# A fused attention and feed-forward block on one core: 32 loads moved to ScalarE's queue, 13 warm-up products instead of 17, and a new written-out order

## The chip, the cores and the metric

The kernel runs on one core of a Trainium2 chip. The metric is the device time of one execution in microseconds (us), lower is better. The kernel before was run three times for its time, and once more with the hardware profiler on. The core has a matrix engine (TensorE, PE in the profile, with its weight loads shown as PEld), a vector engine (VectorE, DVE), a scalar engine (ScalarE, ACT), GpSimd (POOL), and a sync engine (SyncE, SP) that in the kernel before issues all the transfers between memory and the on-chip buffers. Each engine works through its own list of instructions in order; between engines, semaphores hold an instruction back until what it needs is done.

## The reference

One transformer block over 2048 rows of width 576, in bf16: layer norm, a linear-memory attention with 32 heads of width 18 in four segments of 512 rows, an output projection with residual, a second layer norm, and a feed-forward layer of width 4608 with GELU, with residual.

```python
def _A_ref(x, wq, wk, wv, wo, beta):
    # q, k, v = x @ wq, x @ wk, x @ wv, cut into 32 heads and N = 4 segments of L = 512 rows
    g = _sigmoid(beta).reshape(1, H, 1, 1)
    for s in range(N):
        logits = jnp.einsum('bhqd,bhkd->bhqk', qs, ks) * scale + mask
        a_dot = jnp.einsum('bhqk,bhkd->bhqd', _softmax(logits, axis=-1), vs)
        pq = phi(qs)                       # phi(t) = t + 1 where t > 0, else exp(t)
        a_mem = (pq . M) / (pq . z + 1e-06)
        outs.append(g * a_mem + (1.0 - g) * a_dot)
        M = M + einsum(phi(ks), vs); z = z + sum(phi(ks))
    return o @ wo

def _B_ref(x, w1, b1, w2, b2):
    h = _gelu(jnp.einsum('bsd,df->bsf', x, w1) + b1)
    return jnp.einsum('bsf,fd->bsd', h, w2) + b2

h = x + _A_ref(_layernorm(x), ...)
h2 = h + _B_ref(_layernorm(h), ...)
```

## The kernel before

The 2048 rows are cut into 16 tiles of 128 rows (`t`) and 8 chunks of 256 rows (`c`, two tiles each). For a tile, `project` loads its rows (`load_x`, L263), normalises them (`layernorm`), turns them (by TensorE for the first three tiles, L409, by a transposing transfer L154 for the others), and multiplies by wq, wk and wv in column chunks `ch` (L350 is the main part over 4 x 128 rows of the weights, L354 the fifth part of 64 rows, padded with zeros). Chunks 0 and 1 hold 432 columns of q and k, chunk 4 the other 144 columns of both (288 together). `copies` (L502 to L515) takes the products out of the accumulators into `qk_pad` and `v_aug`. Heads are turned once more into `QT` and `KT` (L531, L534). `attend` multiplies scores (L623, 32 rows of the array each, four side by side), takes exp on ScalarE (L627), masks on GpSimd (L631), and weighs values (L639). `output` multiplies by wo, adds the residual, and normalises again. The feed-forward layer follows: `first_layer` (L350 again, with `w1g`, `hT` or `wqkv` as weight buffers, evictions L769 to L771, GELU L792) and `second_layer` (L852, with the residual rows `hc` read back at L843).

The weights of the first feed-forward layer don't stay on the chip: for each group of 512 columns, `load_w1` issues one load of 512 KB (L726) and two of 32 KB (L729, the 64-row rest in two halves, called tails here), into buffers whose last reader must be done. `dma` gives every transfer to SyncE's list.

At the start of the program TensorE has nothing to multiply until the first rows are loaded and normalised. `zeros` (L333) gives it products of a buffer of zeros: 4 of 512 columns and then 13 of 256 columns (`ZEROS = 17` in all), whose result nobody reads. ScalarE meanwhile zeroes padding with copies from the same buffer (`zero`, L308).

Two 64-row products can run side by side in the two halves of the array. `rest_of` pairs such fifth parts (L443 for the projections, L750 for the feed-forward layer). Numbers in the set `WHOLE` name the pairs that are not made; there the fifth part is a full-height product (L354).

Nothing is scheduled when the kernel is built: every operation gets a number as the code defines it, and the table `ORDER` at the end says in which sequence all operations are issued, which fixes each engine's list. `PLACE` gives each accumulator its bank, `FLIP` names the operations that run on their second engine (`alt`) instead of their first. Up to eight transfers are in flight: each takes the next of eight landing semaphores in turn, and waits until the transfer eight places earlier has landed.

## Time and profile before

| | |
|---|---|
| three timed runs | 451.98, 452.14, 453.31 us; median 452.14 |
| the profiled execution | 452.16 us, of which the span from the first to the last instruction is 450.3 us |
| TensorE busy | 445.4 us of the span (99%) |
| ScalarE, VectorE, GpSimd busy | 331.1, 271.4 and 230.2 us |
| transfers | 78.40 MB, mean 174 GB/s |

The profile page lists busy time per engine, the span in 40 slices, the chain of work that ended last, and the costliest groups of instructions. A row of the timeline gives the start, the busy time, the engine and line, what it writes and reads, the size of the array's part that is used (rows x columns, as 128\*128), the shape of one output, how many equal instructions were merged, and in square brackets the idle time before, with what ended it. "SPq" rows are SyncE's issues of transfers, of which only the issue is in the row. Products overlap in the array, so the spacing of starts says more than the length of one.

### The profile page before, as it was taken

Reading aid. Unit: us, or ns where it says so; the run is one execution under the profiler, and the core shown is the slowest. Engines: PE = TensorE matmul, PEld = TensorE weight load, DVE = VectorE, ACT = ScalarE, POOL = GpSimd, SP = SyncE. Lnnn points to the kernel's source line nnn. Section 1 sums busy time; section 2 is a strip of 40 time slices with the busy share of each in tenths; the row PEclk is TensorE's granted clock in tenths of the full one; section 3 lists DMA queues with packets and bytes.
Section 4 is the critical chain, followed back from the end, with each engine's and each line's share of the span. In section 5 each row is a group of like instructions: output and inputs, shape, how many; then the busy total and the mean of one; then the engine's idle time right before and its main releaser. Section 6 shows DMA issues by size and latency. Waiting matters only on the chain.

```text
span 450.3 us, 14470 instructions
## 1 busy us (share of the span) xinstructions
PE 445.4 (99%) x6090; PEld 331.0 (74%) x6090; DVE 271.4 (60%) x624; ACT 331.1 (74%) x318; POOL 230.2 (51%) x409
## 2 busy tenths in 40 slices
PE   8999999999999999999999999999999999999997
PEld 4556877676776777676777677777877878877886
DVE  7989989887887568666666766665523531311231
ACT  8999999988879977889788878587877162352550
POOL 6888865887884667753664784554341002000000
PEclk9999999999999999999999999999999999999999
DMA  7699989678498567796567957585667466365411
GB/s 204 206 209 243 203 215 274 180 194 162 131 168 228 154 148 196 188 155 188 158 153 173 206 123 170 160 227 157 200 181 194 138 192 196 92 191 172 139 41 52
DMA packets 114353, 78.40 MB, mean 174 GB/s; under 512 B 48832, under 2 KB 112240, under 8 KB 114288
## 3 DMA queue, kind: packets, MB, share of 16 engines
q1 hardware_dynamic: 114288, 77.48, 68.7%
q8 instruction: 47, 0.77, 0.7%
q14 instruction: 18, 0.15, 0.1%
HBM read 60.09 MB, written 7.08 MB: 149 GB/s over the span
## 4 chain that ended last, share of the span: by engine, by line
PE 96%; DMA 2%; SPq 1%; issue 0%; DVE 0%
PE bank L350 30%; PE bank L852 25%; PE st L350 10%; PE st L852 6%; PE st L623 6%; PE bank L639 5%; PE bank L683 3%; PE bank L750 3%; PE bank L354 2%; PE st L683 1%; PE st L750 1%; DMA w1g<-in_B_w_dram 1%; PE bank L593 1%; PE bank L531 1%; DMA wqkv<-in_A_wk_dram 1%; PE bank L561 1%
## 5 line engine op out<-in xcount | busy, mean ns | idle before, releaser
L627 ACT ACTIVATE pt<-st 128x2048 bf16<-128x2048 f32 x80 | 150.2, 1877 | 42.4 <-PE st L623 34.8
L852 PEld LDWEIGHTS <-hT 128*128 128x128 bf16 x1188 | 111.5, 98 | 28.1 <-issue 1.5
L852 PE MATMUL bank<-w_sb,hT 128*128 128x288 bf16 (+1 forms) x936 | 130.2, 284 | 0.0
L631 POOL TENSOR_SCALAR_AFFINE_SELECT pt<-pt 128x512 bf16<-128x512 bf16 x128 | 80.5, 644 | 41.2 <-ACT pt L627 40.8
L350 PEld LDWEIGHTS <-w1g 128*128 128x128 bf16 x944 | 86.7, 98 | 18.7 <-issue 7.2
L350 PE MATMUL bank<-xn2T,w1g 128*128 128x256 bf16 (+1 forms) x728 | 89.6, 268 | 0.0
L771 DVE TENSOR_TENSOR hT<-bank,b1T 128x512 bf16<-128x512 f32 x74 | 50.1, 681 | 37.9 <-PE bank L350 36.6
L792 ACT ACTIVATE hT<-hT 128x1536 bf16<-128x1536 bf16 (+4 forms) x25 | 65.9, 2665 | 0.3 <-DVE hT L771 0.2
L769 ACT ACTIVATE hT<-bank,b1T 128x256 bf16<-128x256 f32 x70 | 28.9, 474 | 31.9 <-PE bank L350 31.8
L350 PE MATMUL bank<-wqkv,xT 128*128 128x432 bf16 (+2 forms) x192 | 40.3, 341 | 0.8 <-DMA wqkv<-in_A_wk_dram 0.6
L350 PEld LDWEIGHTS <-xT 128*128 128x128 bf16 x264 | 23.6, 98 | 19.3 <-issue 2.2
L858 DVE TENSOR_TENSOR ot<-bank,hc 128x288 bf16<-128x288 f32 (+1 forms) x26 | 11.7, 448 | 41.9 <-PE bank L852 38.2
L852 PE MATMUL st<-w_sb,hT 128*128 128x288 bf16 (+1 forms) x252 | 33.0, 277 | 0.0
L623 PE MATMUL st<-QT,KT 32*128 32x128 bf16 x1280 | 32.2, 217 | 0.0
L654 DVE STREAM_TRANSPOSE bank<-bank 128x512 f32<-128x512 f32 x32 | 23.0, 720 | 15.0 <-PE bank L639 14.6
L623 PEld LDWEIGHTS <-KT 32*128 32x128 bf16 x1280 | 18.5, 92 | 16.9 <-issue 12.8
L771 DVE TENSOR_TENSOR hT<-st,b1T 128x512 bf16<-128x512 f32 x25 | 16.7, 681 | 23.1 <-PE st L350 23.1
L588 POOL TENSOR_TENSOR pq<-ek,pq 128x512 bf16<-128x512 bf16 x24 | 28.0, 1168 | 4.3 <-DVE ek L587 3.7
L350 PE MATMUL st<-xn2T,w1g 128*128 128x256 bf16 x216 | 29.4, 273 | 0.0
L657 POOL TENSOR_TENSOR r<-r,omg 128x16 f32<-128x16 f32 x32 | 7.0, 219 | 36.9 <-DVE r L655 34.6
L769 ACT ACTIVATE hT<-st,b1T 128x256 bf16<-128x256 f32 x20 | 8.1, 472 | 21.3 <-PE st L350 21.3
L639 PE MATMUL bank<-pt,v_aug 128*19 128x128 bf16 x1280 | 23.8, 220 | 0.0
(157 smaller groups left out, 664.2 us busy)
## 6 DMA issues: line engine op xcount, KB each, us to landing
w1g<-in_B_w_dram SPq DMA_DIRECT2D x57, 512.0 KB, 4.0
w_sb<-in_B_w_dram SPq DMA_DIRECT2D x12, 432.0 KB, 6.3
wqkv<-in_B_w_dram SPq DMA_DIRECT2D x10, 512.0 KB, 4.6
hd<-h_t SPq DMA_DIRECT2D x16, 288.0 KB, 3.4
hc<-hd SPq DMA_DIRECT2D x32, 144.0 KB, 2.3
w1g<-in_B_w_dram SPq DMA_DIRECT2D x114, 32.0 KB, 3.4
x_b<-in_A_x_dram SPq DMA_DIRECT2D x18, 144.0 KB, 2.8
hT<-in_B_w_dram SPq DMA_DIRECT2D x5, 512.0 KB, 5.2
```

The costliest lines, as they stand in the source:

```text
L350: nc.tensor.matmul(out=acc, lhsT=lhsT_of(slice(0, P), k), rhs=rhs_of(slice(0, P), k), start=start and k == 0, stop=False, skip_group_check ...
L588: op(("m_add", n), "POOL", lambda: nc.gpsimd.tensor_tensor(out=pq[:], in0=e_g, in1=pq[:], op=ALU.add), ["ek"], ["pq"])
L623: nc.tensor.matmul(out=st4[:, i, n * P:(n + 1) * P], lhsT=KTs[(2 * s0 + kt) % NK][rows, g, :], rhs=QTs[(2 * c + qt) % NQ][rows, g, :], sta ...
L627: op(("exp", v), "ACT", lambda pt=pt: nc.scalar.activation(out=pt[:], in_=open_four("scores")[:], func=ACT.Exp, scale=scale), [st], [("pt" ...
L631: op(("mask", v), "POOL", lambda n=n, pt=pt: nc.gpsimd.affine_select(out=pt[:, :, n * P:(n + 1) * P], in_=pt[:, :, n * P:(n + 1) * P], pat ...
L639: nc.tensor.matmul(out=bank(ox)[32 * i:32 * i + E, (g % 4) * P:(g % 4) * P + P], lhsT=v_augs[(2 * s0 + kt) % NV][:, G * i + g, :], rhs=pt[ ...
L654: op(("f_T", n), "DVE", lambda: nc.vector.transpose(out=bank(ox), in_=bank(ox)), [], [ox])
L683: nc.tensor.matmul(out=bank(b)[:, 0:HALF], lhsT=xTt[:, k, :], rhs=wo_t[:, k, hs], start=(k == 0), stop=(k == KT - 1))
L769: nc.scalar.activation(out=dst[:, j, :], in_=acc()[:, j, :], func=ACT.Identity, bias=b1T[:, j0 + j:j0 + j + 1], scale=1.0)
L771: op(name, "DVE", lambda: nc.vector.tensor_tensor(out=dst, in0=acc(), in1=bias, op=ALU.add), [tok, "b1T"], keys, alt=("ACT", by_act), afte ...
L792: op(("gelu", c, f0, f), "ACT", lambda: nc.scalar.activation(out=hT[:, f0:f, :], in_=hT[:, f0:f, :], func=ACT.Gelu_apprx_tanh), [], [("hT" ...
L852: nc.tensor.matmul(out=bank(b)[:, 0:w], lhsT=hT[:, q, tl * P:(tl + 1) * P], rhs=w2_sb[:, q, hs], start=(q == 0), stop=(q == NF - 1))
```

## The change

`dma` gets a second engine: with the operation's number in `FLIP`, the same transfer is issued from ScalarE's list (`by_act`) instead of SyncE's. Transposing transfers are left out of that. `FLIP` names 32 transfers: the rows of tile 0 (`x_p`), `beta`, the 576 columns of `wv`, and 29 later ones: 24 loads of feed-forward weights, four of the residual rows `hc` and one store of `out`. The same eight landing semaphores serve both queues. `ZEROS` goes from 17 to 13, which moves all later numbers by four. `ORDER`, `PLACE` and the other entries of `FLIP` are new, and `WHOLE` has 14 entries instead of 13.

```diff
-    ZEROS = 17
+    ZEROS = 13
...
-    def dma(name, kb, desc, issue, rd=(), wr=(), after=()):
-        o = op(name, "SP", issue, rd, wr, after=after)
+    queue = [nc.sync]
+
+    def dma(name, kb, desc, issue, rd=(), wr=(), after=(), turns=False):
+
+        def by_act():
+            queue[0] = nc.scalar
+            issue()
+            queue[0] = nc.sync
+
+        o = op(name, "SP", issue, rd, wr, None if turns else ("ACT", by_act), after=after)
         o.kb, o.desc = kb, desc
         return o
...
-        dma((name, t), 144, 8, lambda: nc.sync.dma_start(out=dst[:], in_=x[t * P:(t + 1) * P, :]), (), [key])
+        dma((name, t), 144, 8, lambda: queue[0].dma_start(out=dst[:], in_=x[t * P:(t + 1) * P, :]), (), [key])
...
     FLIP = {
-        15, 28, 29, 31, 32, 33, 34, 35, 36, 43, 45, 49, 50, 51, 53, 57, 62, 63, 64, 65, 66, 132, 134, 136, 138, 142,
+        0, 9, 14, 15, 25, 29, 31, 32, 33, 34, 35, 36, 38, 46, 49, 50, 51, 57, 58, 59, 66, 125, 128, 130, 132, 134,
...
     WHOLE = {
-        246, 399, 406, 469, 470, 543, 647, 774, 852, 853, 1501, 2141, 2142,
+        242, 243, 395, 402, 465, 466, 539, 643, 770, 848, 849, 1497, 2137, 2138,
     }
...
     ORDER = [
-        23, 57, 24, 42, 54, 25, 0, 29, 58, 30, 26, 28, 59, 27, 38, 125, 67, 68, 126, 69, 70, 71, 6, 22, 127, 1, 72,
+        0, 25, 23, 47, 4, 1, 67, 35, 22, 57, 26, 68, 33, 69, 58, 59, 7, 24, 52, 121, 32, 60, 14, 70, 122, 3, 29, 71,
```

What the new order does is read from the engines' lists. Line numbers of the changed kernel are 10 higher in the functions concerned. The first place is the start of SyncE's list, here of the kernel before (`x_p0`, `x_p1` are the rows of tiles 0 and 1; `128x4x432` is the main part of 432 columns, `64x...` a fifth part):

```order
L263 DMA x_p0_76<-in_A_x_dram 128x576
L273 DMA wqkv_62<-in_A_wk_dram 128x4x144
L263 DMA x_p1_77<-in_A_x_dram 128x576
L263 DMA x_b0_78<-in_A_x_dram 128x576
L281 DMA beta_bc_61<-in_A_beta_dram 128x32
L277 DMA wqkv_62<-in_A_wq_dram 64x576
L273 DMA wqkv_62<-in_A_wq_dram 128x4x144
L277 DMA wqkv_62<-in_A_wk_dram 64x144
L273 DMA wqkv_62<-in_A_wk_dram 128x4x432
```

The same place on SyncE in the changed kernel:

```order
L287 DMA wqkv_62<-in_A_wq_dram 64x576
L273 DMA x_p1_77<-in_A_x_dram 128x576
L287 DMA wqkv_62<-in_A_wk_dram 64x144
L283 DMA wqkv_62<-in_A_wq_dram 128x4x144
L287 DMA wqkv_62<-in_A_wk_dram 64x432
L283 DMA wqkv_62<-in_A_wk_dram 128x4x144
L283 DMA wqkv_62<-in_A_wk_dram 128x4x432
L273 DMA x_b0_78<-in_A_x_dram 128x576
L283 DMA wqkv_62<-in_A_wq_dram 128x4x432
```

The 432 columns of wk are issued ninth before and seventh now; `x_p0` and `beta` have left this list, and `x_b0` (rows of tile 2) comes after them.

The second place is the start of ScalarE's list up to the copy of tile 0's turned rows, `xT0`, for which TensorE's first real products wait. Before (all `L308` rows zero padding; `g_bc` is the gate computed from beta):

```order
L308 ACT_TABLE_LOAD
L308 COPY phik_pad1_93<-pq_116 128x32x14
L308 COPY hT1_126<-pq_116 64x256
L308 COPY hT0_125<-pq_116 128x32x14
L308 COPY MZ_blk_75<-pq_116 128x512
L308 COPY w1g1_67<-pq_116 64x256
L308 COPY phik_pad0_92<-pq_116 128x32x14
```

```order
L336 ACTIVATE g_bc_71<-beta_bc_61 128x32
L308 COPY hT1_126<-pq_116 64x256
L308 COPY MZ_blk_75<-pq_116 128x512
L413 COPY xT0_84<-bank2_152 128x640
L308 COPY hT0_125<-pq_116 128x32x14
L504 ACTIVATE qk_pad0_148<-bank3_153,rs_early0_127 128x16x18
```

Between these two pieces stand two more `w1g` copies. The same stretch of ScalarE's list now:

```order
L273 DMA x_p0_76<-in_A_x_dram 128x576
L318 ACT_TABLE_LOAD
L318 COPY w1g1_67<-pq_116 64x256
L318 COPY hT1_126<-pq_116 64x256
L291 DMA beta_bc_61<-in_A_beta_dram 128x32
L318 COPY MZ_blk_75<-pq_116 128x512
L318 COPY phik_pad0_92<-pq_116 128x32x14
```

```order
L346 ACTIVATE g_bc_71<-beta_bc_61 128x32
L318 COPY hT1_126<-pq_116 64x256
L318 COPY o_nat1_114<-pq_116 128x4x16
L318 COPY MZ_blk_75<-pq_116 128x512
L423 COPY xT0_84<-st0_213 128x640
L283 DMA wqkv_62<-in_A_wv_dram 128x4x576
```

Between these stand a copy each of `hT1`, `phik_pad1` and `o_nat0`. Three issues have come in, two ahead of the `xT0` copy and one right behind it. The computing instructions ahead of that copy are eleven before and now: the 448-element copy into `hT0` and two of 256 into `w1g` have moved behind it, and one of 256 into `hT1` and two of 64 into `o_nat` have come ahead.

The third place is late in the program (segment four, scores of tile 14), on ScalarE. Before, with `pt` the exp of scores, `ek` an exp for the memory part:

```order
L627 ACTIVATE pt1_110<-st_5783 128x2048
L627 ACTIVATE pt2_111<-st_5783 128x2048
L627 ACTIVATE pt3_112<-st_5783 128x2048
L585 ACTIVATE ek_115<-QT2_102 128x512
L627 ACTIVATE pt0_109<-st_5783 128x2048
```

And now:

```order
L637 ACTIVATE pt1_110<-st_5780 128x2048
L853 DMA hc_123<-hd_147 128x288
L736 DMA w1g0_66<-in_B_w1_dram 128x4x512
L637 ACTIVATE pt2_111<-st_5780 128x2048
L595 ACTIVATE ek_115<-QT2_102 128x512
L637 ACTIVATE pt3_112<-st_5780 128x2048
L739 DMA w1g1_67<-in_B_w1_dram 64x256 x2
L873 DMA out_0_dram<-ot_124 128x576
```

Five transfers now stand between the exps, two of them in one place and three in another. TensorE's list keeps its blocks, in another sequence in the first 70 us and from about 285 us on; its runs of equal array shape number 276 before and 272 now, counted over the whole list, and one pair of fifth parts (of tile 3's chunks 2 and 3) is no longer made, so that two full-height fifth parts of 432 columns take its place.

## The prediction

> **What bounds the kernel now.** I read the page's busy shares first, then the table by stage, then TensorE's timeline where that table shows idle time.

> ```profile
> PE 445.4 (99%) x6090; PEld 331.0 (74%) x6090; DVE 271.4 (60%) x624; ACT 331.1 (74%) x318; POOL 230.2 (51%) x409
> PE 96%; DMA 2%; SPq 1%; issue 0%; DVE 0%
> ...
> 0.00:12.00 12.00, 9.97 (x59) 5.45 (x60) 8.63 (x36) 9.80 (x21) 7.27 (x25) 1.00 0.77 213
> 12.00:115.00 103.00, 103.00 (x1804) 72.71 (x1802) 89.63 (x205) 94.45 (x79) 83.36 (x157) 1.00 0.86 204
> 115.00:285.00 170.00, 170.00 (x2436) 123.45 (x2429) 117.50 (x271) 142.49 (x129) 108.58 (x178) 1.00 0.75 173
> 285.00:430.00 145.00, 144.93 (x1627) 114.68 (x1624) 52.23 (x109) 80.54 (x88) 30.94 (x52) 1.00 0.58 169
> 430.00:450.00 20.00, 17.46 (x179) 14.74 (x176) 3.37 (x7) 3.82 (x5) 0.00 (x0) 1.00 0.16 45
> ```

> TensorE carries 96% of the chain, and in the stage table (first busy column: PE) it has no idle time from 12 to 285 us and 0.07 us from there to 430. After its last product only an addition and the last stores are left, and the change leaves those. So loads, exps and evictions hide behind TensorE today. The change can gain only at the start, in that 0.07 us, or in TensorE's own work; it can lose wherever a cover breaks.

> The start, in TensorE's timeline:

> ```profile
> 1.24 3.38 PE L333 MATMUL bank<-pq 128*128 128x512 bf16 x11 [1.24 <-DVE pq L292]
> ...
> 5.12 1.06 PE L333 MATMUL bank<-pq 128*128 128x256 bf16 x4
> 6.20 0.53 PE L409 MATMUL st<-ident,xn 128*128 128x128 bf16 x5
> 6.57 0.38 PE L333 MATMUL bank<-pq 128*128 128x256 bf16 x2
> 7.16 0.67 PE L350 MATMUL bank<-wqkv,xT 128*128 128x288 bf16 x4 [0.21 <-ACT xT L413]
> 7.66 0.29 PE L354 MATMUL bank<-wqkv,xT 128*128 128x288 bf16 x1
> 7.81 0.66 PE L350 MATMUL st<-wqkv,xT 128*128 128x288 bf16 x4
> ...
> 9.15 0.90 PE L350 MATMUL bank<-wqkv,xT 128*128 128x432 bf16 x4 [0.55 <-DMA wqkv<-in_A_wk_dram]
> ```

> Two waits count: 0.21 us for ScalarE's copy `xT0`, and 0.55 us for the 432 columns of wk. The zero products are in idle time. Of the second wait the chain of waits shows the origin: it runs back through SyncE's issues from the first one on.

> ```profile
> 0.79 0.39 SPq L263
> 1.24 0.42 SPq L273
> 1.72 0.50 SPq L263
> ...
> 3.20 0.56 SPq L277
> 3.81 0.58 SPq L273
> 4.42 0.52 SPq L277
> 4.99 4.12 DMA wqkv<-in_A_wk_dram
> ```

> **The change, part by part.**

> *Loads at the start.* The wk load is issued ninth at 4.99 us and lands 4.12 us later, 9.11. In the new list six issues precede it: three fifth parts at about 0.61, 0.57 and 0.57 us from start to start (3.20 to 3.81, and 4.42 to 4.99), `x_p1` at about 0.5 (the row at 1.72), and two of 144 columns at 0.61 and 0.48 (3.81 to 4.42, 1.24 to 1.72). 0.79 + 3.34 = 4.13; I take 4.2. With the same 4.12 us it lands at 8.3. The rows of tile 0 are again the first on their own queue, so I leave their issue at 0.79 and VectorE's start unchanged. No row shows two queues issuing at once. Below, a gain is excluded, since 0.79 is each engine's first moment; above, the two first issues could go one after the other, which shifts everything on SyncE by that row's 0.39 us and lands wk at 8.7. I take 8.3: 0.39 us spread over two queues is the exception, at two of nine issues.

> [...]

> *ScalarE up to `xT0`.* ScalarE now begins with an issue:

> ```profile
> 0.79 1.28 ACT L308 ACT_TABLE_LOAD   x1 [0.79 <-PEq L1056]
> 2.08 0.56 ACT L308 COPY phik_pad<-pq 128x448 bf16<-128x448 bf16 x1
> 2.55 0.87 ACT L308 COPY hT<-pq 64x256 bf16<-64x256 bf16 x2
> ...
> 3.85 0.40 ACT L308 COPY w1g<-pq 64x256 bf16<-64x256 bf16 x1
> 4.15 0.56 ACT L308 COPY phik_pad<-pq 128x448 bf16<-128x448 bf16 x1
> ...
> 6.42 0.68 ACT L413 COPY xT<-bank 128x640 bf16<-128x640 bf16 x1
> ```

> From 2.08 to 6.42 its eleven instructions take 4.34 us. Gone from ahead of the copy are a 448-wide copy (0.47, from 2.08 to 2.55) and two of 256 (0.30 each, 3.85 to the next start at 4.15); new are one of 256 (0.30) and two of 64 elements, which I put at 0.2 each: 4.34 - 1.07 + 0.70 = 3.97 us. Added are two issues of about 0.4 us each, bounded by 0 (hidden while the engine still copies) and 0.8. The first stands ahead of everything and can't hide; of the second I count half: 0.6. Start of the copy: 2.08 + 3.97 + 0.6 = 6.65, end about 7.3, TensorE's first real product 7.4 instead of 7.16 (+0.2). The two 288-column projections then take 1.3 us (7.16 to 7.81, twice), so the 432-column one starts at 8.7, after wk has landed in either case, instead of 9.15: **-0.45 us**. If ScalarE's issues hide, the copy is at 6.05 and wk's landing at 8.3 decides: -0.85.

> *Behind it on ScalarE.* The wv issue (0.58 at most) and three zero copies (about 0.45, 0.45 and 0.3) stand between `xT0` and the eviction for which the turning of q waits. Before, TensorE turned q at once after its projections (13.08 + 0.18 = 13.26, no idle time), so ScalarE is needed there on time. By the same spacings the eviction ends about 0.1 us late: **+0.1**. wv itself is issued near 7.4, ahead of the first projection's end, so I let its users not wait.

> *Zero products.* Four fewer of 0.21 us in time that is idle anyway: nothing, as long as the idle time itself does no harm (rival 1). What covers the cost is the loading and the layer norm of tiles 0 and 1, which end at the same time.

> *TensorE's order.* The products are the same but for fillers and one pair. A block in another array shape costs at its borders:

> ```profile
> 13.08 0.35 PE L354 MATMUL st<-wqkv,xT 128*128 128x432 bf16 x1
> 13.26 1.06 PE L531 MATMUL bank<-ident,qk_pad 128*128 128x128 bf16 x16
> ...
> 17.42 0.40 PE L623 MATMUL st<-QT,KT 32*128 32x128 bf16 x16
> 17.75 0.36 PE L443 MATMUL bank<-wqkv,xT 64*128 64x432 bf16 x2
> 18.04 0.62 PE L531 MATMUL bank<-ident,qk_pad 128*128 128x128 bf16 x8
> ```

> A full product of 432 columns takes 0.18 us (13.08 to 13.26); the pair of L443, side by side, 0.29 (17.75 to 18.04), 0.11 more than one. Sixteen score products, four at a time, are 512 columns' worth, 0.21 us at that rate, and take 0.33: 0.12 more. Four runs of a shape fewer, at 0.12: -0.48. The pair given up costs 2 x 0.18 instead of 0.18: +0.18. Together **-0.3 us**, between 0 (the new borders are the dearer ones) and -0.5.

> *The 29 later transfers on ScalarE.* Each holds its list for about as long as SyncE's:

> ```profile
> 289.06 0.38 SPq L726 DMA_DIRECT2D w1g<-in_B_w_dram  x1
> ...
> 295.22 0.47 SPq L729 DMA_DIRECT2D w1g<-in_B_w_dram  x1
> 295.73 0.60 SPq L863 DMA_DIRECT2D out_dram<-ot  x1
> ...
> 290.19 1.88 ACT L627 ACTIVATE pt<-st 128x2048 bf16<-128x2048 f32 x1 [1.90 <-PE st L623]
> 293.26 1.88 ACT L627 ACTIVATE pt<-st 128x2048 bf16<-128x2048 f32 x1 [1.18 <-PE st L623]
> 296.37 1.88 ACT L627 ACTIVATE pt<-st 128x2048 bf16<-128x2048 f32 x1 [0.72 <-PE st L623]
> ...
> ACT hT L769 <- PE bank L350: 31.8, 12, 12.4
> ```

> 29 x 0.5 is some 14 us of ScalarE, of which 27 fall after 285 us, where the stage table has it busy 80.54 of 145 us and where it waits 0.7 to 1.9 us for TensorE ahead of each of these exps. An issue or two fit into that; so I cost them at **nothing**. If the cover is gone, the exp behind is late, then the mask, then TensorE at L639. Queued behind such an issue on ScalarE are exps, evictions of `hT` and GELU. SyncE gets 32 issues shorter, so a load behind a store on its list goes out earlier.

> Sum: -0.45 + 0.1 - 0.3 = -0.65. The profiled execution, 452.16 (span 450.3 and 1.9 around it), becomes 451.5; it agrees with the median of 452.14, so the forecast is **451.5 us**.

> **The rivals.**

> 1. *Full speed comes later* (slower). The first eleven zero products are 4 x 512 + 7 x 256 = 3840 columns in 3.38 us, 0.22 us for 256; the four of 288 columns from 7.16 to 7.66 make 0.11 for 256. So the array runs at half speed at first, and full speed came about 5.3 us after the first product, by 6.57. Now nine zero products (3328 columns, 2.9 us) begin near 1.5, since VectorE first zeroes a strip of `wqkv`, and TensorE pauses at about 4.4 to 4.6 and 5.6 to 6.05, until the normalised rows are there. If those pauses make the count begin anew at the second turning (6.05), full speed comes at 11.4; half of 7.4 to 11.4 is lost, 2.0 us: 453.5. It decides once full speed comes after 11.4. Against it: the pauses are 0.2 and 0.45 us, and before, 0.21 and 0.55 us of idle time right after release undid nothing. Chance 0.12.
> [...]

> 2. *ScalarE's list is held up* (slower). At the third place three transfers stand in one row, 0.47 + 0.47 + 0.60 = 1.5 us, more than the 1.18 and 0.72 us that exps waited for scores, and each may wait for one of the eight landings. With seven such groups and 0.3 to 0.6 us each on TensorE: +2 to +4, 453.5 to 455.5. For it: the length of the groups. Against: ScalarE's evictions wait for TensorE far longer than its exps (the last row above, up to 12.4 us). It decides when TensorE's idle time from 285 to 430 us exceeds 2 us. Chance 0.14; another 0.04 for a load that comes late in the new order.

> 3. *All of it comes out* (faster). ScalarE's issues hide (-0.85), borders give -0.5 and the 0.07 us goes: -1.4, 450.7. Chance 0.2.

> 4. *The two queues share what there is*, wk lands no earlier and the gap stays: -0.2, 452.0. The loads around it are 144 KB and more, and any faster issue may only queue them. Chance 0.1.

> **How the numbers follow.** A measurement of this kernel tells about 0.3% (1.36 us) from no change. Within it lie the forecast (0.4) and rival 4 (0.1): 0.5. Faster: rival 3, 0.2. Slower: rivals 1 and 2, 0.3. The likeliest case alone spans 451.0 to 452.0. For eight in ten the range takes in most of rival 3 at its low end and the lower half of the slower cases: 450.6 to 454.2.

> **What would show it.** Right: the first `x_p` issue stands on ScalarE near 0.79; the 432-column projection starts near 8.7 with no wait for wk; TensorE is busy all but 0.1 us from 12 to 430 us. Wrong: products of 288 columns near 8 us spaced as zero products are (rival 1); exps late and L639 waiting for L627 or L631 after 285 us (rival 2); a gap ahead of the 432 columns (rival 4).

## The result, and the profile after

| | kernel before | changed kernel |
|---|---|---|
| median of ten executions | 452.52 us (451.98 to 453.72) | 457.25 us (453.22 to 458.69) |
| the profiled execution, and its span | 452.16 us, 450.3 | 458.59 us, 456.9 |

The changed kernel is slower: ratio 1.0096, 95% interval 1.0069 to 1.0123, which is 4.3 us by the ratio and 4.7 by the two medians. The forecast was 451.5 us in a range of 450.6 to 454.2. Its executions also lie further apart, 5.5 us from end to end against 1.7.

The profile page of the changed kernel (busy shares; the chain that ended last), and the same stages as in the prediction:

```profile
PE 447.9 (98%) x6086; PEld 332.8 (73%) x6086; DVE 265.4 (58%) x612; ACT 335.0 (73%) x327; POOL 230.6 (50%) x416
PE 91%; DMA 5%; DVE 2%; POOL 1%; issue 0%; SPq 0%; DVEq 0%; POOLq 0%
...
0.00:12.00 12.00, 9.53 (x43) 5.13 (x43) 7.88 (x28) 8.30 (x18) 7.30 (x28) 1.00 0.75 220
12.00:115.00 103.00, 99.89 (x1691) 69.92 (x1693) 84.60 (x197) 91.14 (x76) 78.72 (x147) 0.98 0.84 200
285.00:430.00 145.00, 144.40 (x1669) 114.08 (x1667) 51.19 (x107) 81.77 (x92) 33.74 (x58) 1.00 0.59 172
```

TensorE, which had no idle time from 12 to 115 us, now has 103.00 - 99.89 = 3.11 us there, and the granted clock of that stage is 0.98 where it was 1.00. Transfers hold 5% of the chain instead of 2%. From 285 to 430 us there are 0.6 us of idle time. TensorE's timeline says where (start, busy time, engine and line, operation, shapes; in brackets the idle time before and what ended it):

```profile
1.64 2.96 PE L343 MATMUL bank<-pq 128*128 128x512 bf16 x9 [1.64 <-DVE pq L302]
4.62 0.71 PE L419 MATMUL st<-ident,xn 128*128 128x128 bf16 x5
5.13 0.63 PE L343 MATMUL bank<-pq 128*128 128x256 bf16 x2
6.57 0.71 PE L419 MATMUL st<-ident,xn 128*128 128x128 bf16 x5 [0.81 <-DVE xn L389]
7.07 0.64 PE L343 MATMUL bank<-pq 128*128 128x256 bf16 x2
7.50 1.17 PE L360 MATMUL bank<-wqkv,xT 128*128 128x288 bf16 x4
...
9.90 1.26 PE L360 MATMUL st<-wqkv,xT 128*128 128x432 bf16 x4
...
12.09 0.61 PE L541 MATMUL bank<-ident,qk_pad 128*128 128x128 bf16 x8
...
34.88 1.39 PE L693 MATMUL bank<-wo_t,xT 128*128 128x288 bf16 x10 [0.57 <-DMA wo_t<-in_A_wo_dram]
36.90 0.35 PE L453 MATMUL bank<-wqkv,xT 64*128 64x432 bf16 x2 [0.30 <-DMA xT<-xn]
...
102.92 1.36 PE L693 MATMUL bank<-wo_t,xT 128*128 128x288 bf16 x5 [2.13 <-DVE ot L868]
...
377.14 0.61 PE L360 MATMUL st<-xn2T,w1g 128*128 128x256 bf16 x4 [0.60 <-DMA w1g<-in_B_w_dram]
```

Both waits of the old start are gone: the first real products (7.50) and the 432 columns (9.90) begin without one. But four products of 288 columns last 1.17 us, where they lasted 0.67: the array is at half speed until 10.63 us (the granted clock's own record), in the kernel before until 6.41. Ahead of that stands a pause of 0.81 us. Then come five waits that were not there: 0.57 for `wo`, 0.30 for a turned tile, 0.11 at 72.5, 2.13 for `ot`, 0.60 for weights. After the longest the granted clock falls to half for 3.41 us, 102.79 to 106.20, which costs half of that, 1.7 us. Such a fall takes the mean granted clock of this execution from 1.000 to 0.996; on record, two of the ten executions have 0.996, this one among them.

The first turning of k marks the end of the start here. In the kernel before it was at 10.99:

```profile
10.99 0.61 PE L531 MATMUL bank<-ident,qk_pad 128*128 128x128 bf16 x8
```

Three parts make up the difference of the two profiled spans, 6.6 us: the first turning of k starts at 12.09 instead of 10.99 (1.1); waits after it 3.7 against 0.07 (3.6); the products themselves 1.85 longer, of which 1.7 is that fall of the clock. At 458.59 us this execution lies near the upper end of its ten, so the typical loss is smaller and need not have the same parts.

### The profile page after: what moved, and what is told of

Read it like the earlier page. It is cut to its first block, busy times and chain, and to the rows that moved or that the text cites. A ratio compares the mean times of both kernels' runs of the same rounds, so it can differ in the third digit from the quotient of the medians.

```text
span 456.9 us, 14478 instructions
## 1 busy us (share of the span) xinstructions
PE 447.9 (98%) x6086; PEld 332.8 (73%) x6086; DVE 265.4 (58%) x612; ACT 335.0 (73%) x327; POOL 230.6 (50%) x416
## 4 chain that ended last, share of the span: by engine, by line
PE 91%; DMA 5%; DVE 2%; POOL 1%; issue 0%; SPq 0%; DVEq 0%; POOLq 0%
PE bank L360 28%; PE bank L862 23%; PE st L360 10%; PE st L862 6%; PE st L633 5%; PE bank L649 4%; PE bank L693 3%; PE bank L760 3%; DMA w1g<-in_B_w_dram 2%; PE bank L364 2%; DMA hc<-hd 1%; DMA xT<-xn 1%; PE st L760 1%; PE bank L603 1%; PE st L693 1%; PE bank L541 1%
## 5 line engine op out<-in xcount | busy, mean ns | idle before, releaser
L781 DVE TENSOR_TENSOR hT<-bank,b1T 128x512 bf16<-128x512 f32 x71 | 48.0, 683 | 46.5 <-PE bank L360 44.5
L360 PE MATMUL st<-xn2T,w1g 128*128 128x256 bf16 x232 | 30.6, 273 | 0.6 <-DMA w1g<-in_B_w_dram 0.6
L693 PE MATMUL bank<-wo_t,xT 128*128 128x288 bf16 x125 | 20.2, 299 | 2.7 <-DVE ot L868 2.1
```

Of the source, the lines that this page charges most:

```text
L360: nc.tensor.matmul(out=acc, lhsT=lhsT_of(slice(0, P), k), rhs=rhs_of(slice(0, P), k), start=start and k == 0, stop=False, skip_group_check ...
L693: nc.tensor.matmul(out=bank(b)[:, 0:HALF], lhsT=xTt[:, k, :], rhs=wo_t[:, k, hs], start=(k == 0), stop=(k == KT - 1))
L781: op(name, "DVE", lambda: nc.vector.tensor_tensor(out=dst, in0=acc(), in1=bias, op=ALU.add), [tok, "b1T"], keys, alt=("ACT", by_act), afte ...
```

## The experiments

The theory formed from this (A): four separate places, each of its own cause, namely the pause at the start, SyncE's stop early on, the residual load at 97 us, and one weight load at 369 us. Against it stand the prediction's step that zero products in idle time can go for nothing, its rival 2 (ScalarE's list), and the rival that the waits only move on. Every ratio below is to the kernel before on the same chip, whose median lay between 452.5 and 452.8 us there; differences between two kernels go by these ratios where nothing else is said. Numbers of operations are the changed kernel's.

**Zero products put back in the pause.** Operation 149 turns tile 1; the later numbers move by four.

```diff
-    ZEROS = 13
+    ZEROS = 17
...
-        ..., 147, 77, 43, 149, ...
+        ..., 151, 77, 43, 80, 81, 82, 83, 153, ...
```

> The changed kernel with four zero products of 256 columns put back, ahead of the turning of tile 1, where TensorE stood idle for 0.81 us; nothing else differs. Theory A (the pauses of the start, not the products, cost time, because the clock is released a window later): release near 7 us instead of 10.6, the pause at 6.57 gone, 1.2 to 1.6 us less than the changed kernel, near 455.8. Rival B (zero products cover nothing but idle time, as the prediction had it): no change, 457.2.

456.32 us, ratio 1.0073 (1.0049 to 1.0096). TensorE's start in it:

```profile
5.09 0.82 PE L343 MATMUL bank<-pq 128*128 128x256 bf16 x6
6.75 0.45 PE L419 MATMUL st<-ident,xn 128*128 128x128 bf16 x5 [0.85 <-DVE xn L389]
...
7.26 0.65 PE L360 MATMUL bank<-wqkv,xT 128*128 128x288 bf16 x4
```

The real products run at full speed from 7.26 on, as theory A has it. But in this execution full speed had come by 5.09, before the four products (six of them take 0.82 us where two took 0.63), so they ran short and the pause stayed; the trace can't say that it was they that helped, and the gain of about 1 us is not clear of the noise, since the two intervals overlap. A cleaner pair follows below (the fifth mend with and without them).

**The padding of `wo` zeroed earlier.** SyncE's and VectorE's lists in the changed kernel:

```profile
7.10 0.51 SPq L273 DMA_DIRECT2D x_p<-in_A_x_dram  x1
11.01 0.34 SPq L298 DMA_DIRECT2D wo_t<-in_A_wo_dram  x1
...
9.30 0.82 DVE L375 BATCH_NORM_STATS2 stats_p<-x_b 128x6 f32<-128x288 bf16 x2 [1.04 <-DMA x_b<-in_A_x_dram]
10.68 0.30 DVE L269 MEMSET wo_t<- 32x288 uint32 x1
```

SyncE issues nothing between 7.61 and 11.01. Its next load, the last 16 rows of `wo`, waits for the zeroing at 10.68, which `FLIP` has put on VectorE, behind statistics that wait for the rows of tile 2. The edit moves operation 15 ahead of those statistics (173):

```diff
-        ..., 150, 82, 83, 173, 174, ..., 148, 87, 15, 131, ...
+        ..., 150, 82, 83, 15, 173, 174, ..., 148, 87, 131, ...
```

> The changed kernel with one operation moved on VectorE: the zeroing of the padding of wo stands ahead of the statistics of tile 2 instead of behind them. Theory A (SyncE's list stands still from 7.6 to 11.0 us, because the load of the last 16 rows of wo waits for this zeroing and VectorE waits for the rows of tile 2): SyncE issues that load by 8.5 us, the waits of 0.57 us for wo at 34.9 and 0.30 us for the turned rows at 36.9 go, 0.9 us less, near 456.3. Rival B (the loads are late since the transfers themselves are slow or are issued in another sequence): the two waits stay, 457.2.

456.76 us, ratio 1.0084 (1.0066 to 1.0102). SyncE goes on at 8.25. The waits become smaller, not zero, and the trace shows why:

```profile
14.94 0.44 SPq L299 DMA_DIRECT2D hT<-in_B_b_dram  x1
19.89 1.32 SPq L164 DMA_TRANSPOSE xT<-xn  x1
...
33.45 1.39 PE L693 MATMUL bank<-wo_t,xT 128*128 128x288 bf16 x10 [0.39 <-DMA wo_t<-in_A_wo_dram]
35.40 0.36 PE L453 MATMUL bank<-wqkv,xT 64*128 64x432 bf16 x2 [0.22 <-DMA xT<-xn]
```

SyncE now stands from 15.4 to 19.9 at the transposing transfer of tile 3, whose rows aren't normalised yet, and the third block of `wo` is listed behind it. Expected were 0.9 us, seen about 0.5 (the intervals overlap): the stop was real, but most of it was hidden by the next one.

**All 29 later transfers back on SyncE** (their numbers out of `FLIP`, the order as it is).

> The changed kernel with the 29 later transfers back on SyncE, each at its place in the written order; the three of the start stay on ScalarE. Rival 2 of the prediction (ScalarE's list is held up by issues): ScalarE is free of 14 us of issues, 2 us or more less, 455 or below. Theory A (only one of them costs, the group of 512 columns issued at 369.33 behind an eviction that waits for TensorE): the wait of 0.60 us at 377 goes, 0.6 less at most, near 456.7. If SyncE's list then becomes the slow one: 457.5 or above, with waits for loads after 285 us.

456.58 us, ratio 1.0098 (1.0067 to 1.0130): no different from the changed kernel. Rival 2 falls. The wait at 377 is gone from this trace, and the one at 102 us (1.49) is there.

**Residual rows earlier.** The chain of waits of the changed kernel ahead of the 2.13 us:

```profile
96.14 0.60 POOL pt L641
96.74 0.22 SPq L702
...
97.05 5.26 DMA hc<-hd
...
102.41 0.47 DVE ot L868
...
102.92 1.12 PE bank L693 x4
```

The load of `hc` (the second half of tile 0's rows, long since stored) is issued at 97.05 behind the store of `h` of tile 2 and takes 5.26 us. In the kernel before it went out 1.9 us ahead of that store:

```profile
92.46 0.52 SPq L843 DMA_DIRECT2D hc<-hd  x1
...
94.34 0.58 SPq L692 DMA_DIRECT2D hd<-h_t  x1
```

The edit moves operation 421 up to where it stood then, behind the transposing transfer 604:

```diff
-        ..., 427, 604, 428, ..., 823, 528, 866, 884, 886, 421, 1080, ...
+        ..., 427, 604, 421, 428, ..., 823, 528, 866, 884, 886, 1080, ...
```

> The changed kernel with one load moved on SyncE's list: the second half of the residual rows of tile 0 goes out ahead of the rows of tile 4 and the store of h of tile 2. Theory A (1.0 to 2.1 us of waiting near 101 us in four profiles come from that place): the wait goes, 1.5 us less than the changed kernel, near 455.8. Rival B (it is a hitch of the transfers, code loading among them, that hits whatever is in flight): another load waits there instead, 457.

455.61 us, ratio 1.0060 (1.0043 to 1.0078), 1.6 us less than the changed kernel (the intervals just overlap). SyncE's list in it:

```profile
95.45 0.52 SPq L853 DMA_DIRECT2D hc<-hd  x1
96.03 0.41 SPq L273 DMA_DIRECT2D x_b<-in_A_x_dram  x1
96.53 0.38 SPq L702 DMA_DIRECT2D hd<-h_t  x1
```

It lands at 97.79, 2.3 us after its issue, and TensorE doesn't wait near 101 us. In the four kernels with the load behind the store that wait was 1.00, 1.48, 1.49 and 2.13 us; in all the others of this order it is absent. The place in the order is the cause; the size differs from execution to execution. Transfers still come near a stop at about 100 us in this kernel too (9 GB/s), but nothing that TensorE needs at once is among them; what slows them is open (last section).

**Four mends together**: the three edits above, and the 512 KB weight load of 369.33 us (operation 2002) back on SyncE.

```diff
     FLIP = {
...
-        ..., 1990, 1993, 2002, 2057, ...
+        ..., 1990, 1993, 2057, ...
```

> The changed kernel with four single mends: the four zero products and the earlier padding as above, the second half of the residual rows of tile 0 loaded ahead of the store of h of tile 2 instead of behind it, and the weight load of 369.33 us back on SyncE. Theory A (four separate causes that add up: 1.5 + 0.9 + up to 3.8 for the stall at 102.9 and the slow clock behind it + 0.6): 451 to 453, as the kernel before or a little under. Rival B (the waits only move to the next late load): 455 or more, with new waits of TensorE in the place of the ones taken away.

453.97 us, ratio 1.0027 (1.0014 to 1.0040): 3.1 us of the changed kernel's 4.3 are back, with no wait at 102 or 377 us and no new one in their place. That is theory A's direction, but short of the 451 to 453 us that it gave. What is left is a wait of 0.92 us at 34 for `wo`, 0.21 behind it, and 0.25 at 16.5.

About the weight load the expectation was wrong in one point. On ScalarE it waited not behind an eviction but for its own buffer, whose last reader ends at 369.30; on SyncE it would have waited as long. The difference is in what overtakes it:

```profile
368.84 0.59 SPq L736 DMA_DIRECT2D wqkv<-in_B_w_dram  x1
...
369.33 0.39 ACTq L736 DMA_DIRECT2D w1g<-in_B_w_dram  x1
```

SyncE, not held up by it, sends another 512 KB 0.5 us ahead, needed later, and the urgent group lands after 7.76 us. With both on SyncE in the listed sequence, in the kernel with four mends, the other goes out 3.2 us behind the urgent group, which lands after 4.6 us. The group was waited for in two of the four traces with this load on ScalarE (0.60 and 0.64 us).

**A fifth mend: `wo` ahead of the transposing transfer.** Operation 18 moves in front of 241.

```diff
-        ..., 256, 532, 241, ..., 469, 217, 18, 275, 537, ...
+        ..., 256, 532, 18, 241, ..., 469, 217, 275, 537, ...
```

> The changed kernel with the four mends and a fifth: the load of wo's third block is issued ahead of the transposing transfer of tile 3, for which SyncE's list waits until 19.9 us, instead of behind it, two other transposing transfers and three loads. If the wait of 0.92 us at 34 us comes from that place in the order: it goes, the one behind it (0.21) too, 1.1 us less than with four mends, near 452.9, as the kernel before. If the transfers as such are slower: the wait stays or goes to another load, 454.

452.86 us, ratio 1.0007 (0.9996 to 1.0019): level with the kernel before, and 0.9 us less than with four mends (the intervals just overlap). The wait for `wo` is gone; the one behind it isn't (0.43 at 35.0). TensorE's start in it:

```profile
6.46 0.45 PE L419 MATMUL st<-ident,xn 128*128 128x128 bf16 x5 [0.55 <-DVE xn L389]
...
7.21 0.67 PE L360 MATMUL bank<-wqkv,xT 128*128 128x288 bf16 x4
...
8.44 0.89 PE L360 MATMUL st<-wqkv,xT 128*128 128x432 bf16 x4
...
10.27 0.61 PE L541 MATMUL bank<-ident,qk_pad 128*128 128x128 bf16 x8
```

**The fifth mend without the four zero products.**

> The kernel with five mends, with 13 zero products again: the four in the pause ahead of tile 1's turning are left out. Theory A (in this order nothing covers a late release of the clock, since the 432 columns of wk no longer wait; in the kernel before a wait of 0.55 us covered most of it): slower by 0.4 to 1.2 us in the median than with 17, near 453.6, with executions both at 452.5 and at 454.5 or above. Rival B (the zero products do nothing here either): 452.9 and the same spread.

454.22 us, ratio 1.0036 (1.0020 to 1.0052), that is 1.3 us more than with them, and the intervals don't touch. Executions lie at 452.95 to 455.95 against 452.49 to 454.26. This is the price of the removed zero products in the new order. The profiled execution of this kernel was its fastest and shows an early release (5.81 us). Of the five traces of the new order with 13 zero products one shows a late release (the changed kernel's), four an early one. So the price is measured, but that it is paid in executions with a late release is inferred from that one trace and from the next experiment's.

**The kernel before with 13 zero products** (the four between the two turnings left out).

> The kernel before with 13 zero products: the four between the turnings of tiles 0 and 1 are left out, all else as it was. TensorE then pauses for some 0.9 us near 5.4 to 6.2 us. Theory A (a pause makes the clock come free a window of 3.41 us later, when the window falls badly, which differs from run to run): slower by 0.3 to 2 us in the median, wider spread, up to 454.5 to 455; the first real product still at 7.2. Rival B (the step of the prediction: idle time is idle time): same time and spread as the kernel before.

453.44 us, ratio 1.0011 (0.9997 to 1.0025): little or nothing, here for rival B by its time. Its trace shows the late full speed and the cover at once:

```profile
6.15 0.71 PE L409 MATMUL st<-ident,xn 128*128 128x128 bf16 x5 [0.87 <-DVE xn L379]
...
7.14 1.14 PE L350 MATMUL bank<-wqkv,xT 128*128 128x288 bf16 x4
...
9.51 0.74 PE L350 MATMUL bank<-wqkv,xT 128*128 128x432 bf16 x3
```

Full speed comes at 9.55 instead of 6.41, the two projections take 2.4 us instead of 1.3, but the 432 columns, which waited 0.55 us for wk until 9.15, are then only 0.36 us late. The old wait paid for the slow clock. The rest of this execution's loss, 1.6 us, is waits of 0.39, 0.76 and 0.44 us at 35.2, 52.8 and 150.0, which have nothing to do with the start.

**The kernel before with only the three loads of the start on ScalarE.** Its own order; operations 0, 9 and 14 in `FLIP`, 0 first in `ORDER`.

> The kernel before, in its own order and with its 17 zero products, but with the three loads of the start (rows of tile 0, beta, wv) issued by ScalarE. The prediction's first term: wk's 432 columns are issued near 4.0 us instead of 4.99 and land near 8.2, the wait of 0.55 us for them goes, ScalarE's copy of tile 0 is 0.2 us later at most: 0.4 us faster, near 452.3 where the kernel before has 452.8. Rival (the two queues share what there is, or the two issues on ScalarE delay its copy by their full 0.8 us): no gain or 0.3 us slower.

454.90 us, ratio 1.0055 (1.0036 to 1.0073): slower by 2.1 us by the medians, where the rival said 0.3.

```profile
1.25 1.28 ACT L316 ACT_TABLE_LOAD   x1 [1.25 <-PEq L1064]
...
7.25 0.68 ACT L421 COPY xT<-bank 128x640 bf16<-128x640 bf16 x1
...
7.99 1.14 PE L358 MATMUL bank<-wqkv,xT 128*128 128x288 bf16 x4 [0.90 <-DMA wqkv<-in_A_wk_dram]
```

ScalarE's issue moves its table load from 0.79 to 1.25 and, with the issue of beta and a wait of 0.29 us for it, the copy of tile 0 from 6.42 to 7.25. The row names a transfer, but the copy ends at 7.93, just ahead of the product. And the clock, released at 4.33, is back at half speed from 7.74 to 11.16 (mean granted clock 0.86 over the first 12 us); TensorE was idle for 48% of the 3.41 us ahead of that. In this trace the start loses 1.6 us (first turning of k at 12.59), and a wait of 1.01 us at 53.6, which the profile puts down to nothing, makes the rest. But only two of the six executions have the mean clock of such a fall (0.996); the other four have 1.000 and are no faster, so what their loss is made of is open.

**The fifth mend with the three loads of the start back on SyncE**, the reverse.

> The kernel with five mends, with the three loads of the start back on SyncE at their places in the order. It prices the prediction's first term in the changed order: wk's 432 columns are issued 0.8 us later (near 5.2) and land near 8.8 to 9.3, the wait for them comes back (0.3 to 0.8 us), ScalarE's list is shorter by two issues: slower by 0.3 to 0.7, near 453.4. Rival (as in the kernel before with only these three loads moved, ScalarE's issue ahead of its table load costs more than the queue gains): faster by 0.5 or more, 452.4.

455.62 us, ratio 1.0061 (1.0049 to 1.0074): 2.4 us slower than with them on ScalarE, far more than the 0.3 to 0.7 expected. TensorE waits in front of its first real products:

```profile
8.64 0.53 PE L360 MATMUL bank<-wqkv,xT 128*128 128x288 bf16 x3 [1.18 <-DMA wqkv<-in_A_wk_dram]
```

The 144 columns of wk are then issued at 4.64 and land at 8.50 (3.75 and 6.84 in the changed kernel). The start accounts for 1.4 of the 2.9 us between the two profiled spans (first turning of k at 11.69 instead of 10.27). Four waits of 0.20 to 0.52 us between 130 and 305 us, which the fifth mend's trace lacks, make up most of the rest, and why they come is open. So in the new order these loads are better on a second queue, and in the old one they are not: queue and order belong together.

**The fifth mend with all later transfers on SyncE.**

> The kernel with five mends, with all later transfers back on SyncE at their places in the order. The prediction's term for them was nothing: 452.9 either way. If ScalarE's issues cost: 0.5 or more less. If the second queue is what keeps loads on time: waits for loads after 285 us, 453.5 or more.

453.03 us, ratio 1.0013 (1.0000 to 1.0027), the same as with 28 of them on ScalarE.

**Two more moves**: the rows of tile 1 (operation 1) ahead of the fifth part of wq (4), and residual rows (283; the expectation calls them tile 3's, they are tile 1's) behind the transposing transfer of tile 5.

> The kernel with five mends and two more moves on SyncE's list: the rows of tile 1 go out first, ahead of the fifth part of wq, and the rows of tile 3 for the residual behind the transposing transfer of tile 5 instead of ahead of it. If both waits come from these places: TensorE's pause of 0.55 us ahead of tile 1's turning shrinks by 0.4 or more, the wait of 0.43 us at 35 goes, 0.4 to 0.8 us less, near 452.2 and under the kernel before (452.8). If not: 452.9 and the waits elsewhere.

453.91 us, ratio 1.0033 (1.0015 to 1.0051): a miss, slower by some 1.2 us (the intervals just overlap). The pause moved forward instead of shrinking:

```profile
5.31 0.61 PE L419 MATMUL st<-ident,xn 128*128 128x128 bf16 x5 [0.72 <-DVE xn L389]
```

Now tile 0's rows are normalised 0.7 us later, with tile 1's rows in flight beside them. The wait at 35 us stayed as well (0.47, now for `h_t`). The start is only 0.2 us later by this; the profile's largest new loss is a wait of 0.84 us at 206 us for a turned tile, whose cause is open.

## Why the prediction was wrong, step by step

Two things that the sum put at nothing failed: the removed zero products, and loads that come late in SyncE's list. By the ratios, 4.0 of the 4.3 us are back with five mends, and single steps account for them: 1.6 (`hc`), 0.9 (`wo`), 0.5 (the zeroing), and 1.0 to 1.3 for the zero products. Each of these is uncertain by up to about 1 us; it is the traces that tie them to their places.

*Loads at the start, -0.45.* The mechanism was right. wk's 432 columns were issued at 4.38 (4.2 forecast) and never waited for; with full speed the 432-column projection starts at 8.44 (8.7 forecast), and the first turning of k at 10.27 instead of 10.99. One thing in it failed. The prediction left "VectorE's start unchanged" and said nothing of tile 1, whose rows, issued earlier than before (1.43 against 1.72), landed later (5.02 against 4.55).

```profile
5.04 0.82 DVE L375 BATCH_NORM_STATS2 stats_p<-x_p 128x6 f32<-128x288 bf16 x2 [0.48 <-DMA x_p<-in_A_x_dram]
```

It comes with the second queue: with the three loads back on SyncE and nothing else changed, the same rows are issued 0.43 us later and VectorE has them 0.3 us earlier (4.50 against 4.81). So it is like rival 4, at a load where it wasn't looked for, though what the two queues share is not shown: in the changed kernel the transfer engines are only 21% busy from 2.7 to 3.3 us. It makes TensorE's pause 0.81 us, where rival 1 had 0.45.

*ScalarE up to `xT0`.* The copy starts at 6.44, forecast 6.65, before 6.42: right within 0.2 us, and the issue of beta runs beside the table load. In the old list (the kernel before with these loads moved) beta is issued later, between copies, and the copy of tile 0 starts at 7.25.

*Behind it on ScalarE, +0.1.* TensorE doesn't wait for ScalarE there in the fifth mend; its first wait after the start is 0.31 us at 16.38, for VectorE.

*Zero products, nothing.* This step failed: 1.3 us. It carried the condition "as long as the idle time itself does no harm", and rival 1 stated the harm, at 2.0 us with full speed from 11.4; the profile has it from 10.63. That a count of 5.3 us begins anew at the second turning was the rival's estimate and is not shown: the turning starts at 6.57, 4.1 us ahead of full speed. A chance of 0.12 was too small. The evidence offered against it, that pauses after release undid nothing, speaks of holding the clock and not of getting it; what the traces show of both is in the last section. The release differs between executions (10.63 us here, 5.81 in the fifth mend with 13 zero products) and may be part of why the changed kernel's times lie so far apart, but not all: with the four products put back they still span 4.1 us.

*TensorE's order, -0.3.* The gain didn't come. From the first turning of k to the last product, waits taken out, TensorE needs 447.46 - 10.99 - 0.07 = 436.4 us in the kernel before, and 436.6 to 436.8 in the five kernels with four mends or more that keep their loads of the start on ScalarE. That would be a loss of 0.2 to 0.4, but the old order with 13 zero products needs 436.7 too, so a loss is not shown. That fewer runs of a shape save 0.12 us each was not borne out, and why is open.

*The 29 later transfers, nothing.* Right, as two pairs show (the changed kernel and the fifth mend, each with these on either queue), with one exception of 0.6 us that comes and goes.

*What was left out.* The largest part is what the prediction gave 0.04: "a load that comes late in the new order". Three places cost about 1.6 (`hc` behind the store), 0.9 (`wo` behind a transposing transfer) and 0.5 us (SyncE held by a zeroing on VectorE). None is on ScalarE's queue, where the prediction looked; all are in SyncE's list, behind something that was not ready. The prediction even noted that SyncE's list gets shorter, as a gain.

Mended at all five places the kernel is level with the one before, not ahead of it. In its profile the start gains 0.7 us; the products take 0.3 more, and waits at 16.4, 35.0, 70.6 and 328.5 us (0.31, 0.43, 0.11, 0.25) take back more than the rest: its span is 451.0 us against 450.3. No version tried beats the kernel before.

## What to carry to other kernels

When a written order changes, go through each in-order list for transfers that wait for something not ready, and price what stands behind them by the time until its first use; here the transfers that changed queue late in the program cost next to nothing, and the loads left behind others cost most (1.6, 0.9 and 0.5 us). Price filler work in idle time before removing it: here the four zero products were worth 1.3 us in the new order, and little or nothing in the old one (ratio 1.0011), where a wait of 0.55 us for wk covered most of the loss; that wait vanished in the same change. Look at what else is in flight beside an urgent load: here the weight load of 369 us landed after 7.76 us in the changed kernel, with another 512 KB sent 0.5 us ahead on the other queue, and after 4.6 us in the kernel with four mends, with both on one queue and the urgent one first.

## What the runs showed of the hardware

Two queues began to issue in the same moment, 0.79 us on ScalarE and 0.80 on SyncE, and their issues took 0.39 and 0.57 us, as they did one at a time on SyncE in the kernel before (0.39 and 0.56). These rows show no delay at the issue. The delay is in the landing: the rows of tile 1 took 3.6 us instead of 2.8.

The transfers of the changed kernel from 99 to 103 us, in 40 slices of 0.1 us:

```profile
GB/s 92 115 104 282 302 291 284 274 275 210 340 74 28 18 0 0 0 0 0 12 0 12 12 12 12 0 12 23 15 18 18 118 358 350 403 369 231 173 357 403
```

For 1.7 us next to nothing moves (0 to 23 GB/s), with at least four transfers under way, among them `hc` and the transposing transfer of tile 8 (97.53 to 102.92). One load of code, 16 KB, lies at its start, 100.05 to 101.01. Shorter quiet stretches stand near this place in other traces, also behind a load of code (down to 9 GB/s with the residual rows earlier, to 10 with the four zero products put back). In the eleven traces of the new order the transposing transfer of tile 8 goes out behind the 288 KB store, a load of code falls into it, and it takes 4.0 to 5.4 us; in the three of the old order it goes out ahead of the store, no load of code starts before its last 0.6 us, and it takes 2.8. Which of these causes the stretches was not tried.

In four of the fourteen traces, of both orders, TensorE stands 0.42 to 1.01 us near 53 us for nothing that the profile names. It may add to the spread of the executions; its cause is open.
